# Batch 0's second transform step in two halves, its rows loaded in three parts, and more second products seeded by ScalarE

## The chip, the cores and the metric

One core of one Trainium2 chip. The metric is device time in microseconds (us) for one launch of the whole program; smaller is better.

## The reference

Eight batches of 4224 positions by 192 channels go through two stages. First a dynamic convolution: seven softmaxed taps per position and head, causal (six zero rows in front). Its output x then goes through a block with a Fourier mix and a normalised two-layer product:

```
mixed = real(fft(fft(x, axis=1), axis=2))
u  = x + mixed
un = (u - mean(u)) / sqrt(var(u) + 1e-6)
out = u + maximum(un @ w_ch1, 0) @ w_ch2      # 192 -> 768 -> 192
```

## The kernel before

**Tiles.** The 4224 positions are 33 rows of 128. A batch has nine groups, c or g: groups 0 to 7 hold four rows each, group 8 one row. All rows of a group sit on the 128 partitions.

**Convolution** (`conv`, batches 0 and 1; `wide_conv` from batch 2). Each of the seven taps of a group is one product, 128x768 (L810 on VectorE, L808 on GpSimd). In batch 0 the seven products of groups 0, 1, 3, 5 and 7 (`PE_SUMS`) are summed by TensorE, by matmuls with the identity into two PSUM banks `pa` (L815, and L772 for taps that ScalarE made in 24-column pieces, L763, as `ACT_TAPS` says); ScalarE copies the sums out (L689). The products of the other groups are added one at a time, by GpSimd (L822), in batch 1 the first of them by VectorE (`DVE_ADDS`).

**First transform step** (`fold`, `spectrum`). GpSimd folds a group's rows with their mirror rows into `sm` (L836, L837), TensorE multiplies by a table into `pg` (L845), ScalarE copies a part (`up`, L851), VectorE makes `gt` (L852, L855), and every second group SP stores `gt` to a DRAM tile `g_d` (L858, L859).

**Second transform step** (`transform`). When all of `g_d` is written, six loads of 112 partitions bring it back transposed as `g2` (L931, L933). 44 matmuls, 99 columns wide for all 17 row pairs, give `pp` (L941), and ScalarE copies each `pp` into `pq` in two or three pieces (L945, L951, L953, L956).

**Mix, norm, product** (`mix`, `norm`, `mlp`). Per group, four matmuls of 97 columns give an even part and an odd part in `eo` (L972); ScalarE copies the odd part (`ot`, L977), VectorE takes difference and sum (L978, L979) and adds both to `u` (L980, L981). The first three groups of batch 0 (`QUICK`) take a short path through normalisation: VectorE statistics, ScalarE scaling to `un` (L1018), TensorE transposes `tr` (L1028), casts to `ht`. Then comes the first product `ph` (L1105) with ReLU evictions `hh`, and the second product `po` (L1149). For the first six groups the second product is in float32, after that in three float16 terms. The end of a tile is either a VectorE instruction u = po * scale + u (L1158), or, from group 10 of the run and for the second tile only (`SEEDED`, `SEED_TILES`), a ScalarE "seed" that writes scaled u into the bank ahead of the matmuls (L1146) and a ScalarE eviction (L1156).

**Weights** arrive as 64-bit words; `words_to_f32` turns each of six pieces into float32 by seven VectorE instructions (L492 to L503), `prep_w1` and `split_f32` make float16 high and low parts.

**Order.** Every engine runs its queue in order. The order is not that of the program text: `plan` prices every instruction (`cost`) and walks through the whole graph; it repeats the walk with ranks from a backward walk (`TURNED`, `PARTS`) and keeps the best order for all five queues. Buffers are by tag: `po` 2 PSUM banks, `fft` 2, `ph` 3; `u` 8 tiles of SBUF. `keep_warm` issues spare matmuls: 40 after group 7 of batch 0 (`WARM`), 8 and 8 between the first mixes (`WARM_EO`).

Of the kernel before, what the change touches and what calls it, by code (L numbers as in the profile page):

```python
# [11 lines left out]
F16 = mybir.dt.float16  # L12
F32 = mybir.dt.float32
# [10 lines left out]
NK1 = 65  # L24
DH = 97
# [11 lines left out]
SPLIT = 4  # L37
# [8 lines left out]
WIRE = 0.7  # L46

F32_GROUPS = 6
WIDE_FROM = 2
SEEDED = 10  # L50
# [18 lines left out]
TURNED = 10  # L69
# [3 lines left out]
PARTS = (1.0, 0.9, 0.7, 0.5)  # L73
LAG = 1000
PATIENCE = {"dve": 120}
# [73 lines left out]
def cost(ins, lane, reads, writes):  # L149
# [10 lines left out]
    if lane == "sp":  # L160
        if ins.opcode == "DmaTransposeAnt":
            return TURN * n / (12 * P), 2000 + 1.2 * n, 1.09 * n
        size, run = BYTES[out.dtype], min(together(ap) for ap in reads + writes)
        return 400, 2000 + WIRE * count(out) * size, out.ap[0][1] * count(out) / run * (0.5 + 0.0023 * run * size)
# [3 lines left out]
    if lane == "pool":  # L168
        t = 183 + (1.92 if out.dtype == F16 else 2.13) * n
        return t - 45, t  # L170
    t = 190 + (0.833 if out.ap[-1][0] == 1 else 1.666) * n + 90 * (len(reads) - 1)
    return (t + 100, t + 90) if len(writes) > 1 else (t - 95, t)


def plan(nc, tc, homes, holds, glued, opening):
# [4 lines left out]
    for at, ins in enumerate(nc.cur_bb.bb.instructions):  # L180
# [14 lines left out]
        for name, spot, w in spots:  # L195
            kind, tag, bufs = homes[name]
            if name not in users and bufs and kind != "dram":
                rows[kind, tag].append(name)
            users[name].append(k)
# [27 lines left out]
    def walk(rank, rows, back=False):  # L227
# [7 lines left out]
        order, table, wire, streamed = {lane: [] for lane in HOP}, None, 0.0, False  # L235
# [17 lines left out]
        for _ in ops:  # L253
# [14 lines left out]
            if lane == "pe" and not back:  # L268
                if mixing[k] and streamed:
                    busy, done = busy - LOADED, done - LOADED  # L270
                streamed = streams[k]
            free[lane], end = now + busy, now + done
# [22 lines left out]
    best = now = walk(list(range(len(ops))), rows)  # L295
    for _ in range(TURNED):
        last = {name: max(now[1][k][1] for k in users[name]) for name in row_of}
        turned = walk([-end for _, end in now[1]], {row: sorted(names, key=lambda name: -last[name]) for row, names in rows.items()}, True)
        if turned is None:
            break  # L300
        late = [turned[0] - end for _, end in turned[1]]
        now = min((w for w in (walk([part * t + (1 - part) * s for t, (s, _) in zip(late, now[1])], rows) for part in PARTS) if w),
                  key=lambda w: w[0], default=None)
        if now is None:
            break
        best = min(best, now, key=lambda w: w[0])
    order = best[2]
# [22 lines left out]
def dft_tables(D):  # L330
# [12 lines left out]
    for kk in range(3):  # L343
        for v in range(N2):
# [6 lines left out]
    te, to = te.reshape(6 * NT, -1), to.reshape(6 * NT, -1)  # L351
    d = np.arange(DH, dtype=np.int64)
# [5 lines left out]
            for m in (f1, te, to, np.concatenate([cm, sm], axis=1))]  # L358
# [3 lines left out]
def tile_dynconv_fnet_mlp(  # L362
# [42 lines left out]
    cs_sb = cpool.tile([DH, 2, DH], F32, name="cs_sb")  # L405
# [3 lines left out]
    ones = cpool.tile([1, P], F32, name="ones")  # L409
    nc.vector.memset(ones, 1.0)  # L410
# [16 lines left out]

    g_ds = [dr.tile([NK1, 2, NT, D], F32, tag=f"g_d{i}", name=f"g_d{i}", bufs=1) for i in range(2)]

    def load_consts():  # L430
        zero = pq[0:NT].rearrange("p e r k -> p (e r k)")[:, 0:2 * D].rearrange("p (k d) -> p k d", k=2)
        nc.gpsimd.memset(zero, 0.0)
        for g_d in g_ds:
            nc.sync.dma_start(g_d[0:NK1:NK1 - 1, 1].rearrange("k t d -> t k d"), zero)
# [3 lines left out]
        nc.sync.dma_start(te_sb, te.rearrange("r (k c) -> r k c", k=3))  # L438
        nc.sync.dma_start(to_sb, to.rearrange("r (k c) -> r k c", k=3))
        csv = cs.rearrange("r (m c) -> r m c", m=2)  # L440
# [14 lines left out]
    def weight_scale(words, bits, nm, other=None):  # L455
# [8 lines left out]
        m2 = cpool.tile([1, 1], F32, name=f"m2_{nm}")  # L464
        row = pst("ph", 3, [P, P], F32, f"mr_{nm}")
# [19 lines left out]
    def words_to_f32(raw, out, nm, bank):  # L485

        hi, lo = raw[:, :, 1], raw[:, :, 0]
        v = nc.vector
        a = pst(*bank, [P, PW], I32, f"pa_{nm}")
        w = pst(*bank, [P, PW], F32, f"pw_{nm}")  # L490
        t = temp(f"t_{nm}", I32)
        v.tensor_scalar(out=a, in0=hi, scalar1=3, scalar2=0x3FFFFFFF,  # L492
                        op0=ALU.logical_shift_left, op1=ALU.bitwise_and)
        v.scalar_tensor_tensor(out=t, in0=hi, scalar=-0x40000000, in1=a, op0=ALU.bitwise_and, op1=ALU.bitwise_or)
        v.tensor_scalar(out=a, in0=hi, scalar1=0x7FF00000, scalar2=None, op0=ALU.bitwise_and)
        v.scalar_tensor_tensor(out=w, in0=a, scalar=float(0x38100000), in1=t.bitcast(F32),
                               op0=ALU.is_ge, op1=ALU.mult)
        v.tensor_scalar(out=a, in0=w.bitcast(I32), scalar1=23, scalar2=23,
                        op0=ALU.logical_shift_right, op1=ALU.logical_shift_left)
        r = t.bitcast(F32)  # L500
        ins = v.scalar_tensor_tensor(out=r, in0=lo.bitcast(U32), scalar=2.0 ** -52, in1=a.bitcast(F32), op0=ALU.mult, op1=ALU.mult)
        out = w if out is None else out
        last_word.append(v.tensor_tensor(out=out, in0=w, in1=r, op=ALU.add))  # L503
        return out
# [21 lines left out]
    def prep_w1(raws):  # L526
# [5 lines left out]
        with held(g2_loads[0, (NK1 + 2) // 3 // TRI * TRI].ins):  # L532
# [12 lines left out]
    def split_w2(_):  # L545
# [7 lines left out]
        for i, both in enumerate((fsc, isc)):  # L553
            nc.vector.tensor_tensor(out=both, in0=scales[0][:, i:i + 1], in1=s2[:, i:i + 1], op=ALU.mult)
# [10 lines left out]
    wm = cpool.tile([P, N2 * H], F32, name="wm")  # L565
# [60 lines left out]
    def conv(b):  # L626

        g_d = g_ds[b % 2]
# [53 lines left out]
        gt, tails, sums, ws_of, firsts = None, [], {}, {}, {}  # L682
        def finish(c, R, u, wp, pa, *_):

            nonlocal gt, done
            if pa:
                n = R * D // 2
# [3 lines left out]
            if R > 1:  # L691
# [625 lines left out]
```

## Time and profile before

| | us |
|---|---|
| median of 3 runs | 1078.33 (1078.23 to 1079.11) |
| span of the profiled execution | 1076.2 |
| what lies around the span, against the median | 2.1 |
| TensorE busy | 1057.1 (98%) |
| VectorE busy | 933.7 (87%) |
| ScalarE busy | 862.9 (80%) |
| GpSimd busy | 851.4 (79%) |

The profile is of one execution. A matmul's duration holds its latency, and matmuls are pipelined, so their rate is read from bursts: duration of a burst less that of one instruction, over the count less one. A float32 matmul of the program is two MATMUL instructions in the trace.

### The profile page before, as it was taken

The page shows a single profiled execution, that of the slowest core. Times are in us where ns is not written, and L with a number is a line of the kernel's source. Part 1 is how long each engine was busy: PE and PEld are TensorE (multiplying, and loading weights), DVE is VectorE, ACT ScalarE, POOL GpSimd, SP SyncE. Part 2 cuts the span into 40 slices and gives each one's busy share as a digit, 9 for nine tenths or more (in the row PEclk, how much of TensorE's full clock was granted, in tenths as well). Part 3 has the DMA queues.
Part 4 walks back from the last instruction along what each step waited for, and adds up shares of the span by engine and source line. Part 5 has one row for each costly group of instructions (what it writes and reads, how often), then busy time and mean ns, then how long its engine had stood idle before and what let it go on. Part 6 is the DMA issues. An engine that isn't in the chain of part 4 may idle for free.

```text
span 1076.2 us, 23645 instructions
## 1 busy us (share of the span) xinstructions
PE 1057.1 (98%) x8603; PEld 803.8 (75%) x8603; DVE 933.7 (87%) x1597; ACT 862.9 (80%) x2597; POOL 851.4 (79%) x616
## 2 busy tenths in 40 slices
PE   8899999999999999999999999999999999999998
PEld 5476687886778777887778777787778777886667
DVE  8999999999989998899989998899989997374433
ACT  4666875669987998889897898889897998699953
POOL 5979899899969999699959999699969999011210
PEclk9999999999999999999999999999999999999999
DMA  9453056624683458625582447734583424523221
GB/s 322 136 147 117 8 136 180 175 48 101 157 233 80 98 133 210 158 75 121 145 215 80 111 127 205 157 76 125 137 180 89 88 68 99 143 56 87 72 71 49
DMA packets 186324, 134.88 MB, mean 125 GB/s; under 512 B 134299, under 2 KB 167008, under 8 KB 186208
## 3 DMA queue, kind: packets, MB, share of 16 engines
q1 hardware_dynamic: 186208, 133.37, 48.3%
q8 instruction: 68, 1.11, 0.4%
q14 instruction: 48, 0.39, 0.1%
HBM read 61.46 MB, written 39.37 MB: 94 GB/s over the span
## 4 chain that ended last, share of the span: by engine, by line
PE 66%; POOL 15%; DVE 10%; issue 5%; ACT 2%; DMA 1%; SPq 0%; POOLq 0%; DVEq 0%; ACTq 0%
PE po L1149 28%; PE ph L1105 24%; POOL u L893 7%; POOL u L822 4%; PE pp L941 4%; PE eo L972 3%; PE ph L1072 3%; PE pg L845 3%; DVE pr L810 2%; POOL sm L836 2%; POOL hl L1048 1%; DVE pr L889 1%; DVE u L889 1%; DMA x_sb<-in_x_dram 1%; POOL hl L1050 1%
## 5 line engine op out<-in xcount | busy, mean ns | idle before, releaser
L893 POOL TENSOR_TENSOR u<-u,pr 128x1536 f32<-128x1536 f32 x144 | 497.1, 3454 | 15.4 <-DVE pr L889 13.4
L1149 PE MATMUL po<-w2h,hh 128*128 128x192 f16 x2880 | 411.2, 246 | 1.3 <-ACT po L1146 0.8
L1149 PEld LDWEIGHTS <-hh 128*128 128x128 f16 x4320 | 364.1, 98 | 61.6 <-issue 18.9
L1105 PE MATMUL ph<-ht,w1h 128*128 128x512 f16 (+1 forms) x1296 | 387.5, 362 | 2.6 <-DVE hh L1125 1.2
L1149 PE MATMUL po<-w2l,hh 128*128 128x192 f16 x1440 | 354.1, 246 | 0.0
L1125 DVE SCALAR_TENSOR_TENSOR hh<-ph,hh 128x512 f16<-128x512 f32 (+1 forms) x396 | 241.3, 634 | 77.5 <-ACT hh L1124 76.9
L889 DVE TENSOR_TENSOR pr<-x_sb,wp 128x1536 f32<-128x1536 f32 x144 | 250.2, 1743 | 6.8 <-POOL u L893 6.7
L1124 ACT ACTIVATE hh<-ph 128x512 f16<-128x512 f32 (+1 forms) x396 | 208.8, 551 | 48.5 <-PE ph L1105 27.1
L1105 PEld LDWEIGHTS <-w1h 128*128 128x128 f16 x1296 | 126.9, 100 | 94.8 <-issue 16.9
L1105 PE MATMUL ph<-ht,w1l 128*128 128x512 f16 (+1 forms) x528 | 180.4, 350 | 0.0
L1038 ACT ACTIVATE un<-u,rs 128x192 f32<-128x192 f32 x252 | 122.0, 539 | 16.4 <-POOL rs L1036 13.1
L1048 POOL TENSOR_TENSOR hl<-un,hl 128x512 f16<-128x512 f32 (+1 forms) x69 | 74.3, 1077 | 74.8 <-ACT hl L1042 39.5
L822 POOL TENSOR_TENSOR u<-u,pr 128x768 f32<-128x768 f32 (+1 forms) x72 | 115.6, 1612 | 8.8 <-DVE rs L1012 4.7
L1009 ACT ACTIVATE junk<-u,st 128x192 f16<-128x192 f32 x252 | 114.2, 453 | 3.0
L1007 ACT ACTIVATE junk<-u 128x192 f16<-128x192 f32 x252 | 90.8, 360 | 21.9 <-DVE u L981 17.5
L972 PEld LDWEIGHTS eo<-cs_sb,pq 97*128 97x128 f32 x544 | 93.4, 191 | 9.0 <-issue 1.1
L972 PE MATMUL eo<-cs_sb,pq 97*128 97x97 f32 x544 | 92.3, 265 | 0.1
L810 DVE TENSOR_TENSOR pr<-x_sb,wp 128x768 f32<-128x768 f32 (+1 forms) x91 | 74.6, 867 | 1.4 <-PE pa L815 0.7
L1105 PEld LDWEIGHTS <-w1l 128*128 128x128 f16 x528 | 52.9, 100 | 23.7 <-issue 3.7
L1036 POOL TENSOR_TENSOR rs<-st,rs 128x4 f32<-128x4 f32 (+1 forms) x69 | 14.0, 202 | 67.8 <-DVE rs L1012 63.1
L836 POOL TENSOR_TENSOR sm<-u 128x382 f32<-128x382 f32 x64 | 64.0, 1000 | 3.4 <-ACT u L689 3.2
L845 PE MATMUL pg<-sm,f_sb 128*128 128x192 f32 x256 | 55.1, 333 | 1.4 <-POOL sm L837 1.3
(143 smaller groups left out, 1585.5 us busy)
## 6 DMA issues: line engine op xcount, KB each, us to landing
out_dram<-u SPq DMA_DIRECT2D x64, 384.0 KB
x_sb<-in_x_dram SPq DMA_DIRECT2D x48, 384.0 KB
g<-g_d SPq DMA_DIRECT2D x40, 336.0 KB
x_sb<-in_x_dram SPq DMA_DIRECT2D x8, 864.0 KB
g_d<-gt SPq DMA_DIRECT2D x32, 195.0 KB
g_d<-gt SPq DMA_DIRECT2D x32, 189.0 KB
w<-in_weight_gen_dram SPq DMA_DIRECT2D x6, 924.0 KB
x_sb<-in_x_dram SPq DMA_DIRECT2D x8, 672.0 KB
```

The lines of the kernel that those rows point to most:

```text
L810: last_product[b] = nc.vector.tensor_tensor(out=dst, in0=rows, in1=wk, op=ALU.mult)
L822: adder.tensor_tensor(out=u, in0=u, in1=pr, op=ALU.add)
L889: last_product[b] = nc.vector.tensor_tensor(out=pr.rearrange("p (s r) (h g) -> p s (r h) g", s=2, g=G), in0=rows, in1=wp[:, :, :, k:k + 1] ...
L893: nc.gpsimd.tensor_tensor(out=u, in0=u, in1=pr, op=ALU.add)
L972: last_mix[b] = nc.tensor.matmul(eo[:, e, j, :], lhsT=pq[0:DH, e, r, r:r + P], rhs=cs_sb[:, e, :], start=True, stop=True)
L1007: nc.scalar.activation(junk, uv[t], AF.Identity, scale=-1.0 / D, accum_out=st[:, t, 0:1])
L1009: nc.scalar.activation(junk, uv[t], AF.Square, bias=st[:, t, 0:1], accum_out=st[:, t, 1:2])
L1038: nc.scalar.activation(un[:, t, :], uv[t], AF.Identity, bias=rs[:, 1, t:t + 1], scale=rs[:, 0, t:t + 1])
L1105: last_ph[n] = nc.tensor.matmul(ph[:, 0:T], lhsT=wt[:, cs_], rhs=ht[:, 0:T, blk], start=(i == 0 and not opens), stop=(i == len(terms) - 1 ...
L1124: nc.scalar.activation(a[:, 0:T], ph[:, 0:T], AF.Relu)
L1125: nc.vector.scalar_tensor_tensor(out=l[:, 0:T], in0=ph[:, 0:T], scalar=0.0, in1=a[:, 0:T], op0=ALU.max, op1=ALU.subtract)
L1149: nc.tensor.matmul(po[t // 2][:, t % 2, :], lhsT=hx[:, t], rhs=wx[:, c2, :], start=(c2 == 0 and i == 0 and not seeds[t // 2] and not (late ...
```

## The change

- The second step of batch 0 gets its own function. `g_d` of batch 0 is three DRAM tiles (`STAGES`: row pairs 0 to 8, 9 to 12, 13 to 16). Three loads per part bring its rows to 54, 24 and 24 partitions of the same three tiles (tag `u`); the first two parts are loaded once group 5 is stored, the last after group 7. Group 6 is stored by itself.
- The near half of the step makes the seven row pairs that the first three groups need: 44 matmuls of 39 columns into four banks, evicted by ScalarE (even) and VectorE (odd). The far half (44 matmuls of 60 columns, ScalarE evictions) stands behind the first three norms.
- Group 6 of batch 0 isn't folded on GpSimd, and group 7 is neither summed nor folded ahead of `pg`: TensorE multiplies the table with near rows, mirrored far rows and their first column, product by product (five pieces: two products, ScalarE's tap, and two sums of two products by VectorE). Its sum for `u` follows behind.
- The mix of the first three groups makes even plus odd on TensorE (194 columns, no copy, no difference and sum).
- `words_to_f32` has four VectorE instructions and two of ScalarE in place of seven of VectorE.
- Seeds from group 3 of the run (`SEEDED`); groups 3 to 9 seed both tiles (`SEED_BOTH`). `DVE_ADDS` gives VectorE a second add for groups 3, 5 and 7 of batch 1. ScalarE's taps: two for groups 1 and 3, one for 5 and 7. Fewer spare matmuls.
- `plan` runs a fixed list of walks with shaken ranks and takes the last; its costs for DMA and for a cold TensorE differ.

```diff
+STAGES = ((0, 9), (9, 13), (13, 17))
-PE_SUMS = {(0, 0), (0, 1), (0, 3), (0, 5), (0, 7)}
+PE_SUMS = {(0, 0), (0, 1), (0, 3), (0, 5)}
+DIRECT = {(0, 7)}
+PAIRS = 2
+ACT_PIECE = 2
+UNFOLDED = {(0, 6)}
-DVE_ADDS = {(1, c): 1 for c in range(2, NC)}
+DVE_ADDS = {(1, c): 1 + c % 2 for c in range(2, NC)}
-SEEDED = 10
+SEEDED = 3
+SEED_BOTH = 10
-ACT_TAPS = {(0, 1): (0,), (0, 3): (0,), (0, 5): (0,1), (0, 7): (0,)}
+ACT_TAPS = {(0, 1): (0, 1), (0, 3): (0, 1), (0, 5): (0,), (0, 7): (0,)}
-WARM = {-1: 14, 7: 40}
-WARM_EO = (8, 8)
+WARM = {-1: 14, 7: 8}
+WARM_EO = (4, 4)
...
-    best = now = walk(list(range(len(ops))), rows)
-    for _ in range(TURNED):
+    now = walk(list(range(len(ops))), rows)
+    for part, spread, seed in TRIALS:
+        shake = [spread * (r - 0.5) for r in draws(seed, len(ops))]
...
-        now = min((w for w in (walk([part * t + (1 - part) * s for t, (s, _) in zip(late, now[1])], rows) for part in PARTS) if w),
...
+        now = walk([part * t + (1 - part) * s + r for t, (s, _), r in zip(late, now[1], shake)], rows)
...
+            if (b, c) in DIRECT:
+                gt = spectrum(b, c, None, gt, pa)
+                banks = [pst("po", 2, [P, 512], F32, f"pa_{b}_{c}_{i}") for i in range(2)]
+                with held(last_pg[0].ins):
+                    for at, both in enumerate(pa):
+                        for bank, rows in zip(banks, both):
+                            nc.tensor.matmul(bank[:, 0:n], lhsT=ident32, rhs=rows.rearrange("p r d -> p (r d)"),
...
+        for i, both in enumerate(pieces or ()):
+            for j in range(J):
+                near, far = both[0][:, j, :], both[1][:, 1 - j, :]
+                parts = ((pg[:, j, :], near), (pg[:, j, 1:D], far[:, D - 1:0:-1]), (pg[:, j, 0:1], far[:, 0:1]))
...
+            if (b, c) == (0, 5):
+                for part in range(len(STAGES) - 1):
+                    load_early(part)
...
+    def load_early(part):
+        lo, hi = STAGES[part]
+        n, g_d = 6 * (hi - lo), g_0s[part]
+        for m0 in range(0, NM, 8):
+            nm = min(8, NM - m0)
...
+            last_g2[0] = nc.sync.dma_start(early[m0 // 8][6 * lo:6 * hi, 0:nm], bass.AP(first.tensor, first.offset, [[D, n], [n * D, nm], [1, D]]))
...
+    def transform_first():
...
+        load_early(len(STAGES) - 1)
...
+        n0 = 2 * QUICK + 1
+        c0, half = NT - n0, NM // 2
+        for m0 in range(0, NM, half):
...
+            for e, (tab, d0) in enumerate(tables):
+                pp = pst(("fft", "po")[e], 2, [P, 3 * half, 2 * n0 - 1], F32, f"pp_0_{m0}_{e}")
...
+                last_pq[0] = place(e, 0, k0, nk, src[:, n0 - 1:2 * n0 - 1], src[:, n0 - 1::-1], (("act", "act"), ("dve", "dve"))[e])
+        yield
+        n1 = NT - n0
+        for m0 in range(0, NM, 8):
...
+                pp = pst("fft", 2, [P, 24, 2, n1], F32, f"pp_0_{m0}_{e}_far")
...
+            if joined:
+                low = eo[:, 0, j, :]
+                where = bass.AP(low.tensor, low.offset, [low.ap[0], [(3 - 2 * j) * DH, 2], [1, DH]])
+                rhs = cs_sb[:, 1:3] if e else cs_sb[:, 0:1].broadcast_to([DH, 2, DH])
...
-                seeds = [late and (i in SEED_TILES or LT == 1) for i in range(2)]
+                seeds = [late and (i in SEED_TILES or LT == 1 or n - 1 < SEED_BOTH) for i in range(2)]
```

## Rows read from the trace of the kernel before

**Rows 1.** Page, part 1: span, and TensorE's share of it

```profile
span 1076.2 us, 23645 instructions
PE 1057.1 (98%) x8603; PEld 803.8 (75%) x8603; DVE 933.7 (87%) x1597; ACT 862.9 (80%) x2597; POOL 851.4 (79%) x616
```

**Rows 2.** Windows: busy us per engine (count), granted clock, DMA share, GB/s

```profile
99.00:300.00 201.00, 196.59 (x1377) 149.52 (x1377) 195.43 (x349) 154.34 (x456) 192.11 (x135) 1.00 0.44 116
300.00:1000.00 700.00, 698.24 (x6124) 537.94 (x6123) 619.13 (x1014) 605.00 (x1799) 572.47 (x400) 1.00 0.51 125
1000.00:1076.00 76.00, 72.90 (x669) 53.70 (x667) 27.22 (x49) 46.59 (x121) 6.84 (x12) 1.00 0.25 68
```

**Rows 3.** Timeline of TensorE: start us, duration us, line, shape, count, idle before

```profile
57.72 2.20 PE L815 MATMUL pa<-pr,ident 128*128 128x384 f32 x6
...
60.41 5.32 PE L815 MATMUL pa<-pr,ident 128*128 128x384 f32 x16
...
67.50 1.46 PE L845 MATMUL pg<-sm,f_sb 128*128 128x192 f32 x8
...
70.87 8.97 PE L563 MATMUL warm<-ident 128*128 128x128 f32 x78
79.69 0.85 PE L941 MATMUL pp<-te_sb,g 102*97 102x99 f32 x8
...
99.23 0.38 PE L1105 MATMUL ph<-ht,w1h 128*128 128x512 f16 x1 [0.56 <-ACT ht L1029]
```

**Rows 4.** The chain that ended last, 60 to 72 us: start us, us, what

```profile
63.10 1.81 POOL u L822
...
69.53 0.90 PE pg L845 x4
...
71.21 0.26 DVE gt L855
```

**Rows 5.** Timelines of VectorE, ScalarE, GpSimd and SP's queue, 60 to 93 us

```profile
62.54 0.95 DVE L810 TENSOR_TENSOR pr<-x_sb,wp 128x768 f32<-128x768 f32 x1 [0.34 <-PE pa L815]
...
92.55 0.56 DVE L980 TENSOR_TENSOR u<-u,eo 128x388 f32<-128x388 f32 x1
...
89.96 0.25 ACT L953 ACTIVATE pq<-pp 97x68 f32<-97x68 f32 x1
...
72.90 1.54 POOL L808 TENSOR_TENSOR u<-x_sb,w 128x768 f32<-128x768 f32 x1 [3.50 <-DVE w L733]
...
71.85 0.32 SPq L859 DMA_DIRECT2D g_d<-gt  x1
75.44 10.26 SPq L931 DMA_DIRECT2D g<-g_d  x6
```

**Rows 6.** Groups by line and shape: count, busy us, mean ns, idle before

```profile
L1149 PE MATMUL po<-w2h,hh 128*128 128x192 f16 x2880 | 411.2, 246 | 1.3 <-ACT po L1146 0.8 <-DVE hh L1125 0.5
...
L822 POOL TENSOR_TENSOR u<-u,pr 128x768 f32<-128x768 f32 x60 | 108.6, 1817 | 5.9 <-DVE rs L1012 4.7
...
L845 PE MATMUL pg<-sm,f_sb 128*128 128x192 f32 x256 | 55.1, 333 | 1.4 <-POOL sm L837 1.3
...
L815 PE MATMUL pa<-pr,ident 128*128 128x384 f32 x120 | 44.0, 511 | 5.6 <-DVE pr L810 5.5 <-POOL pr L808 0.2
...
L941 PE MATMUL pp<-te_sb,g 102*97 102x99 f32 x336 | 37.9, 251 | 0.3 <-ACT pq L956 0.2
...
L1158 DVE SCALAR_TENSOR_TENSOR u<-po,isc,u 128x384 f32<-128x384 f32 x61 | 37.1, 608 | 14.5 <-PE po L1149 14.1
...
L1146 ACT ACTIVATE po<-u,fsc 128x384 f32<-128x384 f32 x55 | 31.9, 580 | 8.7 <-DVE u L1158 8.3
...
L498 DVE TENSOR_SCALAR pa_w<-pw_w 128x384 int32<-128x384 int32 x6 | 3.4, 560 | 0.1
```

**Rows 7.** Windows around a pause of TensorE early in the run, columns as in rows 2

```profile
8.00:11.00 3.00, 0.51 (x2) 0.38 (x3) 2.35 (x7) 2.11 (x11) 1.90 (x3) 1.00 1.00 409
11.00:15.00 4.00, 4.00 (x9) 2.21 (x8) 4.00 (x5) 3.45 (x18) 1.85 (x4) 0.57 1.04 404
```

More of the change, by code (lines that the diff above doesn't have):

```diff
@@ L72 @@
 NEAR = 1500
-PARTS = (1.0, 0.9, 0.7, 0.5)
 LAG = 1000
+COLD = 2600
+WINDOW = 5000
 PATIENCE = {"dve": 120}
@@ L271, in walk @@
                 streamed = streams[k]
+            if lane == "pe" and not back:
+                if now > free[lane] + COLD:
+                    slow = now + WINDOW
+                if now < slow:
+                    busy, done = 2 * busy, done + busy
             free[lane], end = now + busy, now + done
@@ L681, in conv @@
             return
-        gt, tails, sums, ws_of, firsts = None, [], {}, {}, {}
+        gt, tails, sums, ws_of, firsts, kept = None, [], {}, {}, {}, []
         def finish(c, R, u, wp, pa, *_):
             nonlocal gt, done
+            n = R * D // 2
+            if (b, c) in DIRECT:
[5 more added lines that the diff above has]
+                            nc.tensor.matmul(bank[:, 0:n], lhsT=ident32, rhs=rows.rearrange("p r d -> p (r d)"),
+                                             start=(at == 0), stop=(at == len(pa) - 1))
+                for i in range(2):
+                    nc.scalar.copy(u[:, i].rearrange("p r d -> p (r d)"), banks[i][:, 0:n])
+                done += R
+                return done / N2
             if pa:
-                n = R * D // 2
                 for i in range(2):
@@ L811, in conv @@
                         products.append(last_product[b].ins)
-                    if pa:
+                    if direct:
+                        pa.append((pr[:, 0], pr[:, 1]))
+                        left = K - len(at) - len(kept)
+                        if left % 2 == 0 and left < 2 * PAIRS:
+                            pa.pop()
+                            both, more = (q.rearrange("p r d -> p (r d)") for q in kept[-2:])
+                            nc.vector.tensor_tensor(out=both, in0=both, in1=more, op=ALU.add)
+                    elif pa:
                         n = R * D // 2
@@ L837, in fold, with spectrum @@
         last_fold[b] = nc.gpsimd.tensor_tensor(out=sm[:, :, 0], in0=a[:, :, 0], in1=z[:, ::-1, 0], op=ALU.add)
-    def spectrum(b, c, sm, gt):
-        J, g_d = (2 if c < NC else 1), g_ds[b % 2]
+    def spectrum(b, c, sm, gt, pieces=None):
+        J = 2 if c < NC else 1
         t2 = 2 * c + 1 if c < NC else 0
-        pg = pst("po" if (b, c) == (1, 0) else "fft", 2, [P, 2, D], F32, f"pg_{b}_{c}")
-        for j in range(J):
+        bank = ("po", 2) if (b, c) == (1, 0) else ("ph", 3) if (b, c) in DIRECT else ("fft", 2)
+        pg = pst(*bank, [P, 2, D], F32, f"pg_{b}_{c}")
+        for i, both in enumerate(pieces or ()):
+            for j in range(J):
+                near, far = both[0][:, j, :], both[1][:, 1 - j, :]
+                parts = ((pg[:, j, :], near), (pg[:, j, 1:D], far[:, D - 1:0:-1]), (pg[:, j, 0:1], far[:, 0:1]))
+                for n, (dst, rows) in enumerate(parts):
+                    last_pg[b] = nc.tensor.matmul(dst, lhsT=f1_sb[:, t2 + j, :], rhs=rows, start=(i + j + n == 0),
+                                                  stop=(i == len(pieces) - 1 and n == 2), skip_group_check=True)
+        for j in range(J if not pieces else 0):
             last_pg[b] = nc.tensor.matmul(pg[:, j, :], lhsT=f1_sb[:, t2 + j, :], rhs=sm[:, j, :], start=True, stop=True)
@@ L1205, in queue @@
                 f(arg)
-    add(0.0, 1.0, transform(0))
-    run()
+    first_half = transform_first()
+    next(first_half)
     with held(last_up[0].ins):
```

218 lines of the change are left out of this document (142 added, 76 removed).

## The prediction

> **What bounds the kernel now.** I read the page's busy shares first [rows 1]: TensorE is busy for 98% of the span, no other engine for over 87%. A busy share can hide stages, so the windows come next [rows 2]. From 99 us on TensorE is idle for 4.4 us up to 300, for 1.8 us in the next 700, and for 3.1 us in the last 76: 9.3 us in all. What stands ahead of 99 us is the opening, in which TensorE mostly serves others: the first matmul of the first product starts at 99.23 [rows 3]. So the time is the opening plus the matmul work behind it plus some 9 us of gaps. An edit pays if it brings that first matmul forward, and costs what matmul work it puts behind it. Work taken off VectorE or GpSimd pays only where TensorE waits for them, and between 99 and 300 us they are busy for 195.4 and 192.1 of 201 us, so they are near the bound there too.
>
> The sum is made against the profiled execution, span 1076.2 us; the median of the runs, 1078.33, lies 2.1 above it, which I add unchanged.
>
> **The opening, term by term.** The marks of before are: last `gt` done 71.47 [rows 4], second step's loads issued from 75.44 [rows 5], first `pp` 79.69 [rows 3], last copy into `pq` done 90.21, first add to `u` 92.55 [rows 5], first product 99.23.
>
> *Last gt.* Three engines end close together. VectorE's last product ends at 63.49 and GpSimd's last sum (group 6) at 64.91; then come the folds and group 7's `pg`, 69.53 to 70.43 [rows 4, 5]. That looks like 5 us to be had by dropping folds. But TensorE works without a pause to speak of from 57.72 [rows 3]. From a burst, less one instruction's own duration [rows 3, 6], a sum instruction comes every (5.32 - 0.51)/15, about 0.33 us, four per product, so the seven products of group 7 cost 28 x 0.33 = 9.2 us; a 192-column one of `pg` every (1.46 - 0.33)/7 = 0.16 us, a 128-column one 8.97/78 = 0.115 us. A piece of the new group 7 is two tiles of four wide instructions and two of one column. For one column I take 0.115 us, as for 128 (below, nothing; above, the 0.16 of 192 columns). That is 2 x (0.64 + 0.23) = 1.7 us, five of them 8.7. Group 6 unfolded adds 1.7 - 0.65 = 1.1. So TensorE's work here stays: -9.2 + 8.7 + 1.1 = +0.6. It starts some 0.9 us sooner (one product fewer for VectorE in groups 1 and 3 each, one more in 5), and about 0.8 us of the wait for copy and fold goes. Term -1.1. Bounds: 0, if TensorE's queue takes it all, and -3.5, if it clears early and group 6 binds (64.91, piece 1.7, then the same 1.04 from `pg` to `gt`, about 67.9). The two pair sums (2 x 0.95) lie in place of the waits for a bank before products [rows 5].
>
> *Store to load.* 75.44 - 71.47 = 3.97 us. Half the bytes in the last store: between 3.0 and 4.0, I take 3.5, as the wait is mostly not bytes. Term -0.5.
>
> *Load to first pp.* 4.25 us, with 336 KB per load and several in flight. Now three loads of 147 KB or less; parts one and two went ahead. Between 2.2 and 4.25 I take 3.25. Term -1.0. On SP's queue the six early loads (0.33 us each, 2 us) wait for group 5's store and stand near the last stores; a slip there costs up to 2 us, which is kept for the range. The Trainium skill ("DMA: Bandwidth & Descriptors", the section on why a DMA increments its semaphore by 16) says that a DMA from SP uses the largest number of engines up to 16 that divides its outer size. By that, 24 rows run on 12 engines, 54 on 9, against 16 for 112 rows. This speaks against the parts: as an estimate, a third more time for the moving bytes would take half of this term, for a total 0.5 us higher.
>
> *Second step.* 79.69 to 90.21, 10.5 us. Its 88 instructions of 99 columns come every (0.85 - 0.25)/7 = 0.086 us [rows 3, 6], 7.6 us, and the rest is waiting for loads and for ScalarE to free two banks. With 39 columns the spacing lies between 0.034 (in proportion) and 0.086 (if something other than columns sets it); I take 0.06: 5.3 us. Four banks, so no wait for one. The last eviction adds about 0.7 (two copies; 0.25 us for 68 elements [rows 5], some 0.35 for 230); even and odd go out on two engines. 6.0 us, term -4.5 (bounds -6.8 and -2.2).
>
> *Mix of group 0.* From the last copy to the first add, 2.34 us, with a copy, a difference and a sum between. Now eight instructions of 194 columns, at 0.168 each 1.3 us, part of them ahead of the last eviction, and straight into the add. Term -1.1, and -0.2 for instructions of group 1 that no longer stand between. Weight preparation loses three VectorE instructions of 0.56 us on each of six pieces [rows 6], 10 us; with them in place it would have held this start, so it is a condition, not a term.
>
> Sum of the opening: -1.1 - 0.5 - 1.0 - 4.5 - 1.3 = -8.4; the first product starts near 90.8.
>
> **Behind the start.** The far half is another 88 instructions. 60 columns: between 0.052 and 0.086 us, I take 0.06, 5.3 us. Joined mixes add 24 x (0.168 - 0.115) = 1.3. Sixteen fewer spare instructions between the mixes give back 16 x 0.115 = 1.8. Net TensorE work +4.8 from the second step on. All of it counts, because the wait for the norm shrinks as well and has no other gap left.
>
> Costed at nothing, with their cover: 13 VectorE endings of 0.61 us become 26 ScalarE instructions of 0.58 (groups 3 to 9), 15 us on ScalarE, which has 47 us idle between 99 and 300 [rows 2, 6]; without it each seed would stop TensorE. Three adds of 1.82 us go from GpSimd to VectorE [rows 6], covered by what VectorE loses (8 us of endings, weight work). Far evictions, 14 copies of some 0.35 us, go to the same idle time of ScalarE. The sum of group 7 (20 x 0.33 = 6.6 us) and 8 spare pairs fill the DMA wait, where 78 spare instructions, 9 us, stand now [rows 3]. Steady batches 2 to 7 are unchanged but for their order.
>
> 1078.3 - 8.4 + 4.8 = **1074.7 us**.
>
> **Rivals.**
> - *Batch 1's rows hold the gain.* TensorE comes to batch 1 sooner, but GpSimd, busy for 192 of 201 us, starts that batch's sums at 72.90 for VectorE's tap tables [rows 2, 5]. If that start stays, it gains only the three adds, 5.4 us, which would do; if VectorE is late with them, none, and the 3.6 us become waits: 1076 to 1078.3, say 1077. For: the near-full window. Against: VectorE is relieved more than it is given. Chance 0.15.
> - *The opening clears early.* `gt` at the -3.5 bound and spacing by columns: -2.4 and -2.3 more, 1070.0. For: folds and copies really go from the chain. Against: TensorE's unbroken run from 57.72. Chance 0.2.
> - *Seeds stop TensorE; slower.* A bank must now be evicted, seeded and handed over before the first matmul of a tile. The one such wait of before took 0.8 us [rows 6]. If all 13 new seeds cost that, +10.4: 1085. It decides from 5 such waits on (+4, gain gone). Against: 55 seeds cost 0.8 us together. Chance 0.08.
> - *The clock falls in the DMA wait.* After TensorE had worked 0.51 of 3 us, the granted clock was 0.57 over the next 4 us [rows 7], the lower level of 1.2 GHz for most of them. If it falls ahead of the near half, that and the first mix double, +6.6: 1081. The Trainium skill ("TensorE: Matmul & The Clock Gate", the part on the HAM clock gate) says that the slow level is the default and that activity lifts it; the trace agrees. Against: 6.6 us of sums plus spare work in that wait. Chance 0.04.
> - *It doesn't do what it says*: a part's loads or SP's order hold the near half, so load and step gain nothing but columns: about +2, 1076.7. Chance 0.08.
>
> **How the numbers follow.** The forecast has the rest, 0.45, with 1072 to 1076.2 as its own range. A measurement of this kernel tells about 0.2%, 2.2 us, from no change: below 1076.2 is faster, above 1080.5 slower. Faster: most of the forecast, the early case and a small part of the others, 0.74. Same: most of batch 1's hold and of the case where loads don't come early, with the forecast's upper tail, 0.16. Slower: seeds and clock with part of their tails, 0.10. Range 1067 (early case with a cheap far half) to 1079 (the holds with a slip on SP's queue).
>
> **What the changed profile would show.** Right: first product near 91; a near half of about 6 us; store to first `pp` under 7.2 us in place of 8.2; no pause of TensorE before seeded tiles; idle after the start still near 9 us. Last `gt` before 68 speaks for the early case, after 71 against my first term. Wrong: a first product later than 95, over 13 us of idle between 99 and 300, or a granted clock below 1.00 behind 60 us.

## The result, and the profile after

The changed kernel takes 1085.87 us (median of four runs, 1084.76 to 1088.02), against 1078.72 for the kernel before in the same session: ratio 1.007, 95% interval 1.0056 to 1.0085. It is 0.7% slower, clear of the noise, and outside the range that was given. The profiled execution took 1088.02 us with a span of 1086.2, and the sums below are made against that span; it is the slowest of the four, so they overstate the median's loss by some 2 us.

First the timeline of TensorE (start, duration, line, shape, count, idle time before it):

```profile
79.96 0.38 PE L506 MATMUL me_w<-m_w,ones_w 1*128 1x1 f32 x2
82.47 14.54 PE L1016 MATMUL pp<-first_tables,g 102*97 102x39 f32 x88 [2.13 <-issue]
97.69 5.25 PE L1111 MATMUL eo<-cs_sb,pq 97*128 97x194 f32 x16 [0.68 <-ACT pq L1028]
...
103.44 1.48 PE L1111 MATMUL eo<-cs_sb,pq 97*128 97x194 f32 x8
...
108.45 2.96 PE L1016 MATMUL pp_far<-first_tables,g 102*97 102x60 f32 x32
...
112.00 1.51 PE L1016 MATMUL pp_far<-first_tables,g 102*97 102x60 f32 x16
113.35 0.38 PE L1247 MATMUL ph<-ht,w1h 128*128 128x512 f16 x1
...
114.83 1.32 PE L1016 MATMUL pp_far<-first_tables,g 102*97 102x40 f32 x14
```

Three things stand against [rows 3]. The first `pp` starts at 82.47, not 79.69, behind a pause of 2.1 us that was not there before. The near half takes 14.54 us, 0.16 us per instruction, almost twice what its twin, the far half, takes in the same trace (2.96 us for 32). And sixteen joined mixes take 5.25 us, while the next eight take 1.48. The windows say why (columns as in [rows 2]; the granted clock is the third column from the right):

```profile
60.00:80.00 20.00, 19.70 (x111) 16.06 (x109) 14.51 (x29) 9.75 (x34) 15.18 (x11) 1.00 0.60 179
82.00:84.00 2.00, 1.53 (x10) 1.56 (x10) 1.61 (x4) 0.57 (x1) 2.00 (x2) 0.51 1.04 221
84.00:90.00 6.00, 6.00 (x39) 6.00 (x38) 0.00 (x0) 2.57 (x7) 6.00 (x5) 0.50 0.89 293
90.00:97.00 7.00, 7.00 (x44) 6.88 (x43) 2.65 (x7) 1.02 (x2) 7.00 (x5) 0.50 0.04 9
98.00:102.00 4.00, 4.00 (x13) 4.00 (x13) 2.61 (x6) 2.34 (x6) 4.00 (x4) 0.50 0.00 0
103.00:200.00 97.00, 95.74 (x596) 75.66 (x595) 92.98 (x192) 71.89 (x200) 77.86 (x63) 1.00 0.32 94
```

From 82 to 102 TensorE runs at the lower level, 1.2 GHz; between its first pause, which is like that of [rows 7], and 1085 us it does so nowhere else. In this run the clock fell at the pause, ahead of the near half. Note that the busy column says 6.00 of 6 and 7.00 of 7: a busy share doesn't show a halved clock.

GpSimd's last sum of group 6 and VectorE's last `gt` come late already (67.8 and 72.2 us):

```profile
65.34 2.46 POOL L883 TENSOR_TENSOR u<-u,pr 128x768 f32<-128x768 f32 x1
...
71.85 0.34 DVE L924 TENSOR_TENSOR gt<-pg,up 128x190 f32<-128x190 f32 x1
```

The rest of the late rows is on SP's queue and in the chain of waits. Both are shown around the last stores (the first fence is SP's timeline, the second the chain):

```profile
72.22 0.30 SPq L933 DMA_DIRECT2D g<-gt  x1
72.97 0.27 SPq L934 DMA_DIRECT2D g<-gt  x1
73.61 2.80 SPq L1010 DMA_DIRECT2D g<-g  x3
...
78.66 1.16 SPq L1010 DMA_DIRECT2D g<-g  x3
```

```profile
67.56 6.03 DMA g<-gt
...
73.61 0.30 SPq L1010
...
73.96 6.48 DMA g<-g
80.44 2.02 issue
```

The last store is issued at 72.97 and the loads that need it at 78.66, 5.7 us later; before it was 71.85 and 75.44 [rows 5], 3.6 us. The store of group 5 lands 6.03 us after its issue. What ran beside these stores are the early loads. The chain names a load of part two and leaves the 2.02 us behind it open ("issue"). By the steps of the loads' semaphores, which the trace also records, it is part three's first load, issued at 78.66, that lands last ahead of the first `pp`, at 82.27.

What did go well stands behind the first mix:

```profile
99.00:300.00 201.00, 197.63 (x1392) 155.95 (x1391) 188.78 (x348) 160.07 (x462) 177.50 (x128) 0.99 0.38 99
300.00:1000.00 700.00, 699.44 (x6164) 544.89 (x6163) 621.73 (x1027) 607.61 (x1818) 582.10 (x402) 1.00 0.51 129
1000.00:1086.00 86.00, 83.19 (x748) 60.34 (x745) 31.43 (x56) 54.82 (x146) 8.82 (x15) 1.00 0.25 65
```

TensorE's idle time is 3.4, 0.6 and 2.8 us, together 6.8 where [rows 2] had 9.3, and GpSimd has 177.5 us of work in the first window where it had 192.1.

### The profile page after: what moved, and what is told of

The parts are those of the page before. It is cut to its first block, busy times and chain, and to the rows that moved or that the text cites. A ratio compares the mean times of both kernels' runs of the same rounds, so it can differ in the third digit from the quotient of the medians.

```text
span 1086.2 us, 23835 instructions
## 1 busy us (share of the span) xinstructions
PE 1066.8 (98%) x8667; PEld 824.3 (76%) x8667; DVE 917.8 (84%) x1566; ACT 881.0 (81%) x2657; POOL 847.7 (78%) x611
## 4 chain that ended last, share of the span: by engine, by line
PE 81%; DVE 9%; DMA 3%; POOL 3%; ACT 2%; issue 2%; SPq 0%; POOLq 0%; ACTq 0%
PE po L1292 33%; PE ph L1247 29%; PE eo L1111 5%; PE pp L1055 5%; PE ph L1214 4%; PE pg L914 3%; DVE pr L864 3%; POOL u L883 2%; DVE pr L967 2%; PE pp L1016 1%; DVE hh L1267 1%; DMA x_sb<-in_x_dram 1%; PE pp_far L1016 1%; ACT pr L809 1%; DMA g<-g 1%
## 5 line engine op out<-in xcount | busy, mean ns | idle before, releaser
L1292 PE MATMUL po<-w2h,hh 128*128 128x192 f16 x2880 | 423.5, 246 | 0.0
L1292 PEld LDWEIGHTS <-hh 128*128 128x128 f16 x4320 | 368.8, 98 | 65.4 <-issue 16.5
L1247 PE MATMUL ph<-ht,w1h 128*128 128x512 f16 (+1 forms) x1296 | 393.7, 362 | 1.9 <-DVE hh L1267 1.8
L883 POOL TENSOR_TENSOR u<-u,pr 128x768 f32<-128x768 f32 (+1 forms) x69 | 111.6, 1622 | 22.7 <-issue 15.2
L1190 POOL TENSOR_TENSOR hl<-un,hl 128x512 f16<-128x512 f32 (+1 forms) x69 | 74.3, 1077 | 57.5 <-issue 28.2
L1111 PEld LDWEIGHTS eo<-cs_sb,pq 97*128 97x128 f32 x544 | 101.9, 195 | 9.4 <-ACT pq L1028 0.8
L1111 PE MATMUL eo<-cs_sb,pq 97*128 97x97 f32 (+1 forms) x544 | 99.1, 271 | 0.8 <-ACT pq L1028 0.7
L864 DVE TENSOR_TENSOR pr<-x_sb,wp 128x768 f32<-128x768 f32 (+1 forms) x84 | 68.3, 860 | 2.1 <-POOL u L883 1.2
```

What stands on the lines that cost most here:

```text
L864: last_product[b] = nc.vector.tensor_tensor(out=dst, in0=rows, in1=wk, op=ALU.mult)
L883: adder.tensor_tensor(out=u, in0=u, in1=pr, op=ALU.add)
L1111: last_mix[b] = nc.tensor.matmul(where, lhsT=pq[0:DH, e, r, r:r + P], rhs=rhs, start=not joined or e == 0, stop=not joined or e == 1)
L1247: last_ph[n] = nc.tensor.matmul(ph[:, 0:T], lhsT=wt[:, cs_], rhs=ht[:, 0:T, blk], start=(i == 0 and not opens), stop=(i == len(terms) - 1 ...
L1292: nc.tensor.matmul(po[t // 2][:, t % 2, :], lhsT=hx[:, t], rhs=wx[:, c2, :], start=(c2 == 0 and i == 0 and not seeds[t // 2] and not (late ...
```

## The experiments

In all but the thin spares and the last two, the order of all engines is that of the changed kernel but for the edit named; spare matmuls and moves on SP are put in behind the planner. Times of before in these sessions were 1078.3 to 1078.6.

**A bridge over the pause.** If the pause lowered the clock, work in it should keep it.

```diff
+ for _ in range(10):   # ahead of the first matmul of the near half
+     nc.tensor.matmul(warm_bank, lhsT=ident32, rhs=ident32)
```

> The changed kernel with ten more spare 128-column matmuls of TensorE right ahead of the near half, every other instruction in the same order. They fill the pause of 2.13 us (80.34 to 82.47) behind which the granted clock fell to 0.50 for 20.5 us. Theory A, the clock costs the time: clock 1.00 from 14 us on, near half about 7.3 us in place of 14.5, first mix 2.7 in place of 5.3, time 1074 to 1078, below the kernel before. Theory B, the loss lies in the new order and work behind the opening: the time stays within 2 us of the changed kernel's 1085.9 even if the clock holds. Theory A2, the pause does not matter, because the near half's 39-column matmuls alone lose the clock: it falls a few us into the near half, time 1080 to 1086.

Measured: 1083.77 us, ratio to before 1.0046 (1.0029 to 1.0063). The near half, and windows:

```profile
82.30 10.57 PE L1024 MATMUL pp<-first_tables,g 102*97 102x39 f32 x88
```

```profile
80.00:86.00 6.00, 6.00 (x65) 6.00 (x65) 3.30 (x10) 1.90 (x6) 6.00 (x5) 1.00 1.04 280
87.00:92.00 5.00, 5.00 (x33) 5.00 (x33) 1.77 (x5) 1.31 (x3) 5.00 (x4) 0.50 0.40 94
```

The pause is gone and the clock falls all the same, inside the near half. So the pause decides when it falls, not that it falls. This is the third theory, A2. The near half, at full clock for its first part, takes 10.57 us in place of 14.54.

**The loads of x later.** Five loads of batch 1's rows that stood behind the last parts go behind the weight copies on SP.

```diff
- g2 loads, x_sb loads, w1 copies
+ g2 loads, w1 copies, x_sb loads
```

> The changed kernel with five loads of x for batch 1 moved on SP's queue from ahead of the eight small copies of the first weights to behind them; no other instruction moves. In the changed kernel they were issued from 79.87 us, while the last rows of the second step were still landing (82.27). If these loads hold up the rows: first matmul of the near half 1 to 2 us earlier, at 80.5 to 81.5, the pause of TensorE under 1.2 us, and the clock may stay at 1.00, then 1075 to 1079. If the rows are held up by their own packets or engines: first near-half matmul within 0.4 us of 82.47, clock lost as before, 1084 to 1088.

Measured, one execution: 1083.37 us; the first `pp` starts at 81.40, 1.1 us sooner, and the clock still falls. Some 0.4 us of that are there already at the last stores (71.80 in place of 72.22), so about 0.7 us are the loads': those of the next batch took some part in holding the rows up.

**Thin spares in the kernel before.** In the kernel before, the spare matmuls of the DMA wait move one column instead of 128.

```diff
- nc.tensor.matmul(spare, lhsT=ident32, rhs=ident32)
+ nc.tensor.matmul(spare[:, 0:1], lhsT=ident32, rhs=ident32[:, 0:1])
```

> The kernel before with its 40 spare matmuls ahead of the second step cut from 128 columns to one column; same number, same order. TensorE issues just as many instructions there but streams next to nothing. If instructions alone keep the clock: granted clock 1.00 throughout, time within 2 us of 1078.5. If the clock needs the columns: it falls to 0.50 between 74 and 80 us, the second step of the kernel before takes longer than its 10.5 us, and the time rises by 3 to 10 us, to 1082 to 1088: that is then the price of the clock in the old structure.

Measured, one execution: 1085.11 us beside 1078.58 for before. The windows, and below them that of the kernel before over the same wait:

```profile
60.00:72.00 12.00, 11.75 (x54) 8.15 (x52) 10.52 (x25) 10.30 (x40) 7.21 (x9) 1.00 0.39 136
73.00:80.00 7.00, 7.00 (x35) 7.00 (x34) 6.90 (x19) 0.58 (x1) 7.00 (x5) 0.50 0.62 165
```

```profile
72.00:80.00 8.00, 8.00 (x75) 8.00 (x74) 7.90 (x21) 0.90 (x3) 7.10 (x5) 1.00 0.63 167
```

This is the clearest of all: TensorE is issued without a gap, 35 instructions in 7.00 of 7 us, and the clock is halved, where the kernel before, busy for 8.00 of 8 us, keeps 1.00. The weights are 128 columns wide in both; the spares move one column in place of 128. The price in the old structure is 6.5 us, but it doesn't lie where the expectation looked for it. The timeline of the run:

```profile
75.70 10.38 PE L564 MATMUL warm<-ident 128*128 128x1 f32 x48
85.94 1.61 PE L942 MATMUL pp<-te_sb,g 102*97 102x99 f32 x8
...
96.90 2.21 PE L973 MATMUL eo<-cs_sb,pq 97*128 97x97 f32 x16
```

At the lower level the one-column spares take about 0.22 us each (10.38 over 48), against 0.115 for 128 columns at full clock [rows 3], and the second step, which stands behind them in the queue, starts at 85.94 in place of 79.69: 6.2 us. From there to the first mix it is only 1.0 us longer (10.96 in place of 9.94).

**Columns into the near half.** Ten spares as above, the loads of x later, and behind every second matmul of the near half a spare of 83 columns into the unused end of its bank.

```diff
  for i, mm in enumerate(second_step(pp, rows_of, near, d0, m0, half)):
+     if i % 2 == 1:
+         nc.tensor.matmul(bank[0:83, 429:512], lhsT=ident32[:, 0:83], rhs=ident32[:, 0:83])
```

> The changed kernel with ten spare matmuls ahead of the near half, a spare matmul of 83 columns behind every second one of the near half's 44 (20 in all, into unused columns of the same banks), and the five loads of x moved behind the weight copies on SP. The rest of the order is as it was. Clock theory: the pause alone was not the cause, the near half itself is (39 columns moved for 97 columns of weights leave TensorE idle inside). With the spares in it the granted clock stays at 1.00; the near half takes 88 x 0.083 + 40 x 0.072 = 10.2 us in spite of the added work, the first mixes 2.9 us in place of 5.3 to 5.5; first ph near 106, time near 1080.7. Rival, rows that land late or something else but the clock sets the near half's pace: near half 10.6 + 2.9 = 13.5 us, mixes as before, time 1085 or more.

Measured: 1081.68 us, ratio 1.0026 (1.0015 to 1.0036). Start and end of the near half, and windows:

```profile
82.47 0.46 PE L1032 MATMUL pp<-first_tables,g 102*97 102x39 f32 x4
...
92.64 0.46 PE L1032 MATMUL pp<-first_tables,g 102*97 102x26 f32 x4
```

```profile
80.00:93.00 13.00, 13.00 (x150) 12.97 (x150) 5.88 (x17) 4.20 (x10) 13.00 (x9) 1.00 0.53 140
94.00:97.00 3.00, 3.00 (x10) 3.00 (x10) 1.94 (x5) 2.42 (x6) 3.00 (x3) 0.50 0.35 135
```

The near half with 40 more instructions in it takes 10.6 us, at full clock, where the changed kernel takes 14.54. The bridge alone gave 10.57, so inside the near half the spares cost what they save; what they add is that the clock is still high at its end. It falls for about 3 us behind the wait before the first mix, so it did not stay at 1.00 throughout. The clock theory's sums come near (it had 10.2 us and 1080.7), and the rival's 13.5 us and 1085 fall.

**Partitions of the parts.** The parts padded to 64, 32 and 32 partitions, with zero rows in the tables.

```diff
- early[m0 // 8][6 * lo:6 * hi, 0:nm], bass.AP(..., [[D, n], [n * D, nm], [1, D]])   # n = 54, 24, 24
+ early[m0 // 8][p0:p1, 0:nm], bass.AP(..., [[D, p1 - p0], [n * D, nm], [1, D]])     # 64, 32, 32
```

> The changed kernel with the three parts of the rows padded to 64, 32 and 32 partitions (zero rows in the tables), so 18 to 33% more bytes per load; order of all engines as it was. Theory that the number of partitions of a load (54 and 24) keeps DMA engines idle: the store of group 5 lands in under 5.5 us in place of 6.0, the last rows 1 to 2 us earlier than 82.3, time 1083 to 1085. Rival, latency and the waits in SP's queue set it, not the spread over engines: last rows at 82 or later, time 1085.5 to 1087.

Measured: 1085.54 us, ratio 1.0062 (1.0047 to 1.0077). With 18 to 33% more bytes the last parts are issued at 77.34 in place of 78.66 and the first `pp` starts at 81.49 in place of 82.47. That is what the first theory wants of the rows, but the time isn't told apart from that of the changed kernel. It leans to the theory and settles nothing.

**Where the loads stand on SP.** Two runs. In the first the two loads of part one that stand between the stores go behind the last store; in the second only the last six loads are turned to go tile by tile. Here p2.t0 is part two's load into the first of the three tiles; p1.t0 goes ahead of all of these.

```diff
- stores g4/5, p1.t1, p1.t2, stores g6, stores g7, p2.t0, p2.t1, p2.t2, p3.t0, p3.t1, p3.t2
+ stores g4/5, stores g6, stores g7, p2.t0, p1.t1, p2.t1, p3.t0, p3.t1, p1.t2, p2.t2, p3.t2      (first run)
+ stores g4/5, p1.t1, p1.t2, stores g6, stores g7, p2.t0, p3.t0, p2.t1, p3.t1, p2.t2, p3.t2      (second run)
```

> The changed kernel with the two loads of the first part that stand between the stores moved behind the last store, and all loads behind it in the order of the tiles. Theory that the early loads slow the stores down: the store of group 5 lands in 3 to 4 us in place of 6.0, first pp at 79.5 to 80.5 in place of 82.5, and the time falls by as much, 1083.5 to 1084.5, with the clock still low in the near half. Rival, stores land late for their own reasons (many small packets): first pp at 82 or later and the time within 1 us of 1085.9.

> The changed kernel with the six last loads on SP turned from part two (three tiles), part three (three tiles) to tile by tile: the first tile's part two and part three, then the second tile's, then the third's. Nothing else moves. Theory that the loads of part two that run beside the last store hold it up (5.4 us to landing in the changed kernel, 2.9 us in the run where no loads ran beside it): now one load of part two runs beside it, the first tile's part three is issued near 76.5 in place of 78.7 and the first pp starts at 80 to 81 in place of 82.5; time 1083.5 to 1084.5, the clock still low in the near half. Rival, the store lands late whatever runs beside it, or the rows land late for the bytes ahead of them: first pp at 82 or later, time 1085.5 to 1086.5.

Measured: 1086.55 us (1.0076, 1.0061 to 1.0091) and 1085.64 us (1.0069, 1.0054 to 1.0083). SP's timeline of the first run:

```profile
72.68 0.32 SPq L945 DMA_DIRECT2D g<-gt  x1
73.53 1.93 SPq L1021 DMA_DIRECT2D g<-g  x3
...
75.62 1.99 SPq L1021 DMA_DIRECT2D g<-g  x5
```

The load that waits for the last store is issued 2.9 us after it, not 5.7. So the loads of part one did hold the store up. But its tile now queues behind three other loads, it lands 7.1 us after its issue in place of 3.6 (by its semaphore), and the first `pp` starts at 82.82: what was won at the store was lost at the bytes ahead. In the second run the wait for the store stays (72.71 to 77.95), so part two is not what held it. The first `pp` starts at 81.19, then waits 0.5 us in the half. Each theory was half right.

**All repairs.** Loads tile by tile, x later, two spares ahead, twelve in the near half (behind every third matmul), four in the wait before the first mix. The second run of this kind also moves part one's two loads behind the first tile's last part.

```diff
+ stores g4/5, p1.t1, p1.t2, stores g6, stores g7, p2.t0, p3.t0, p2.t1, p3.t1, p2.t2, p3.t2      (first run)
+ stores g4/5, stores g6, stores g7, p2.t0, p3.t0, p1.t1, p2.t1, p3.t1, p1.t2, p2.t2, p3.t2      (second run)
```

> All repairs together on the changed kernel: loads tile by tile as in the run before, the loads of x behind the weight copies, two spare matmuls ahead of the near half, one spare of 83 columns behind every third matmul of the near half (12), and four in the wait before the first mix. Theory that clock and late rows are the whole loss: first pp near 80.3, near half 7.3 + 12 x 0.144 = 9.0 us, first mix at 90, granted clock 1.00 (or low for 4 us at most), first ph near 103.3 and with 972.6 us behind it a span near 1076, time 1077 to 1078.5: at or below the kernel before. Rival, that the two-half step is slower by itself: time over 1080 with the clock at 1.00 throughout.

> The run with all repairs, but the two loads of part one that stand between the stores go behind the last store too, and behind the first tile's loads: first tile part two, part three, then the second tile's three parts, then the third's. Theory that the loads of part one, 54 partitions and 0.58 MB, are what holds the last store up (landing 5.4 us after issue with them, 2.9 without): first tile's part three is issued near 75.6 and the first pp starts near 80, 1.5 us sooner than in the run before; with the clock at 1.00 time 1078.5 to 1079.5. Rival, the same bytes now come behind the store and the near half waits for the second and third tile: first pp sooner, but waits of 1 us or more inside the near half and no gain, 1080 or more.

Measured: 1081.84 us (1.0046, 1.0025 to 1.0068) and 1078.94 us (0.9999, 0.9988 to 1.0011). The first is not steady: six of its twelve executions took 1079.2 to 1080.8, two about 1083 and four 1087.5 to 1089.8, at a mean granted clock of 0.989 to 0.991 in those four. Its profiled execution took 1080.43 us at a mean clock of 0.998, but the first `pp` still waited for its rows until 81.47; so its expectation, 1077 to 1078.5, was missed. The second took 1078.3 to 1080.0 in all ten, as expected, at 0.997 to 1.00. TensorE's timeline of the second, SP's and the windows:

```profile
80.69 0.63 PE L1041 MATMUL pp<-first_tables,g 102*97 102x39 f32 x6
...
89.97 0.80 PE L1111 MATMUL pp<-ident 128*83 128x83 f32 x8
90.80 2.90 PE L1145 MATMUL eo<-cs_sb,pq 97*128 97x194 f32 x16
...
104.19 0.38 PE L1281 MATMUL ph<-ht,w1h 128*128 128x512 f16 x1
```

```profile
72.43 0.32 SPq L959 DMA_DIRECT2D g<-gt  x1
...
74.51 3.29 SPq L1035 DMA_DIRECT2D g<-g  x7
```

```profile
80.00:90.00 10.00, 10.00 (x119) 9.98 (x119) 5.85 (x17) 4.18 (x10) 10.00 (x8) 1.00 0.46 100
90.00:100.00 10.00, 9.86 (x83) 9.36 (x83) 9.97 (x39) 7.20 (x19) 10.00 (x7) 1.00 0.51 183
```

The load that waits for the last store is issued 2.1 us after it, the first rows are there when TensorE's spare work ends, and the clock stays at 1.00. The same three groups of loads in another order and 18 spare matmuls take the whole loss away, and no more than that.

**Rows in time, no spares.** The same order on SP, not one spare matmul added.

> The changed kernel with the loads moved as in the last run of all repairs (five loads of part one and two behind the last store, first tile first; x behind the weight copies) and not one spare matmul added. Theory that the 39-column near half lowers the clock by itself, pause or not: TensorE runs into the near half at 80.3 with no pause to speak of, the granted clock falls 2 to 6 us into it all the same, near half 10 to 12 us, first mixes at half speed, first ph near 107, time 1081.5 to 1083.5, so 3 to 4.5 us are the clock's where the rows are in time. Rival, the clock falls only behind a pause of TensorE: clock 1.00 throughout, near half 7.3 us, no spares to pay for, time 1076.5 to 1077.5, faster than both kernels.

Measured: 1083.21 us (1.004, 1.0029 to 1.0052). Timeline and windows:

```profile
79.84 0.38 PE L519 MATMUL me_w<-m_w,ones_w 1*128 1x1 f32 x2
80.15 1.74 PE L1029 MATMUL pp<-first_tables,g 102*97 102x39 f32 x18
82.17 8.70 PE L1029 MATMUL pp<-first_tables,g 102*97 102x39 f32 x70 [0.29 <-issue]
91.54 4.90 PE L1124 MATMUL eo<-cs_sb,pq 97*128 97x194 f32 x16 [0.68 <-ACT pq L1041]
```

```profile
80.00:85.00 5.00, 4.71 (x54) 4.61 (x54) 3.69 (x11) 2.52 (x7) 5.00 (x4) 1.00 0.55 126
86.00:91.00 5.00, 4.87 (x30) 4.74 (x30) 1.57 (x5) 1.12 (x3) 5.00 (x4) 0.50 0.49 123
```

TensorE runs into the near half without a pause worth the name (0.29 us in it) and the clock falls in it, as expected. With the near half as it is the clock falls with or without a pause ahead of it; the rival would have given 1076.5 to 1077.5. The last run of all repairs differs from this one by its 18 spares alone, and they are worth some 4 us: 1078.94 in place of 1083.21, with 1078.52 and 1078.58 for before in their sessions.

**Two controls with a new order.** The first is the kernel before with only the seeds of the change; the second the changed kernel with the old second step in one piece and everything else kept. Both change the count of operations, so the planner orders everything anew.

```diff
- SEEDED = 10                                                  (on the kernel before)
+ SEEDED = 3; SEED_BOTH = 10
```

```diff
- first_half = transform_first(); next(first_half)             (on the changed kernel)
+ add(0.0, 1.0, transform(0)); run()      # one DRAM tile, six loads of 112 partitions
```

> The kernel before (its own second step, no parts, its own planner) with only the seeds of the change: from group 3 of the run, both tiles for groups 3 to 9. The planner makes a new order. Theory that the seeds are worth something behind the start: the opening stays (first ph 98 to 101), TensorE's idle time between 99 and 300 us falls from 4.4 to 2 or 3, time 1076 to 1077.5. Rival, TensorE is bound by its own work and idle time goes elsewhere: 1078 to 1079. Seeds that stop TensorE: over 1081, with idle time before the second product's matmuls.

> The changed kernel with the second step of batch 0 as it was before, in one piece of 99 columns with six loads of 112 partitions and one DRAM tile; everything else of the change stays (group 7 multiplied product by product, group 6 unfolded, joined mixes, shorter weight preparation, seeds from group 3, two added adds on VectorE). Two spare matmuls more ahead of it. The planner makes a new order from nine walks. Theory that halves and parts are what costs, and the rest is worth 2 to 3 us: last gt at 71 to 72.5, first pp near 80, granted clock 1.00 behind 15 us, first ph near 98, idle of TensorE behind it 7 us or less, time 1075 to 1077. Rival, the rest of the change is worth nothing without the halves, or only in the order that was chosen for it: 1078 to 1081.

Measured: 1085.97 us (1.0069, 1.0052 to 1.0086) and 1080.93 us (1.0023, 1.0014 to 1.0033). Neither tells what it was made for. In the first, TensorE waits near 190 us for a weight that VectorE makes late in the new order, and the clock falls there as well (wait, then window):

```profile
PE ph L1106 <- DVE w2l L553: 3.8, 1, 3.8
```

```profile
192.00:199.00 7.00, 5.81 (x15) 2.86 (x15) 6.09 (x11) 2.86 (x5) 4.92 (x9) 0.52 0.66 198
```

In the second the same weight costs 2.3 us, in the profiled run with no such fall; by its number it falls to its rival (1078 to 1081). An order found for other work isn't a control. What the seeds or the rest are worth by themselves stays open.

## Why the prediction was wrong, step by step

The forecast span was 1076.2 - 8.4 + 4.8 = 1072.6, the measured one 1086.2, 13.6 more. Cut at two marks (the forecast's marks are 79.69 - 2.6 = 77.1, and 6.0 us behind that):

| us | before | forecast | after | all repairs |
|---|---|---|---|---|
| start to first `pp` | 79.69 | 77.1 | 82.47 | 80.69 |
| first `pp` to first mix | 9.94 | 6.0 | 15.22 | 10.11 |
| first mix to end | 986.6 | 989.5 | 988.5 | 987.1 |

The forecast's second mark is the last copy into `pq`, which in before ends 0.6 us behind the start of the first mix. Of the 13.6 us, 5.4 lie ahead of the first `pp`, 9.2 between it and the first mix, and the rest came out 1.0 us under the forecast.

- **The clock rival, given a chance of 0.04, is what happened.** It cost 14.54 - 7.5 = 7.0 us in the near half and 5.25 - 2.90 = 2.35 in the first mixes, 9.4 together (7.5 is 88 times the 0.085 of the far half, 2.90 the mixes at full clock in the repaired run). With the rows in time and no spares it still cost 10.7 - 7.5 = 3.2 and 4.90 - 2.90 = 2.0 us. The rival's sum was +6.6. Its mechanism was half right: it looked for idle time in the DMA wait and found cover there, and as the rows came late, the cover ran out and a pause of 2.1 us did come; but without the pause the clock falls too, in the middle of a near half that TensorE works through without a gap. The step that failed is the sentence against it, "6.6 us of sums plus spare work in that wait", which looked at the time ahead of the near half and not at the near half itself.
- **The rows came 5.4 us later than forecast.** Last `gt` was done at 72.2, not 70.4: GpSimd's last sum of group 6 ended at 67.8, where before it ended at 64.9, and 22 instructions of `pg` stood behind it. This is outside the bounds of that term, which held that GpSimd's sums would end as before. Store to load took 6.5 us from the last `gt`, not 3.5; the forecast took the early loads to have gone ahead. Those of part one were in the store's way, and those of part two were issued behind it (73.61). The slip "of up to 2 us" on SP's queue was looked for in issue time; it lay in the transfers. Load to first `pp` took 3.8, not 3.25. So the rival "It doesn't do what it says", given 0.08, came true as well: the parts' loads held the near half, by 3.5 us in these two terms where it had about 2.
- The sentence from the Trainium skill ("DMA: Bandwidth & Descriptors", the section on why a DMA increments its semaphore by 16) spoke against the parts and was priced at 0.5 us. The run with 64 and 32 partitions agrees in direction (rows 1.0 us sooner with more bytes). The steps in which a load's semaphore rises agree with the counts of engines: behind one at the issue there are 12 for 24 partitions and 9 for 54, and there are 16 in all for 112, 64 or 32.
- **Spacing of the second step.** Taken as 0.06 us, it is 0.085 in the far half ((1.51 - 0.25)/15 to (2.96 - 0.25)/31) with 60 columns, (1.32 - 0.25)/13 = 0.082 with 40, and (1.74 - 0.25)/17 = 0.088 with 39 in the run of rows in time, before the clock falls; so it does not go by columns here: the upper bound, 0.086, was the value, 2.2 us more in each half. Before, 99 columns cost the same 0.086 [rows 3, 6]: two halves load the same weights twice, and the split of the columns saves nothing.
- **Behind the first mix** the forecast was too dear. With 2.35 of clock and 2.2 of spacing taken out, the rest is 5.6 us under it. 2.5 of that are idle time (9.3 to 6.8), which the forecast kept whole. The other 3 or so lie between the first mix and the first products, and were not taken apart. The mark "first product near 90.8" failed for one more reason: the forecast put the far half behind the first product, and in the trace 64 of its 88 instructions stand ahead of it. It starts at 113.35, and at 104.19 with all repairs.
- **With all repairs** the span is still 5.3 us over the forecast: 3.6 ahead of the first `pp`, 4.1 between it and the first mix (2.2 of spacing, some 1.9 of spares), and 2.4 under it behind. So the gain that was forecast is not there with the two losses taken away either.
- The other rivals fell. The opening did not clear early. Batch 1's rows held nothing, with GpSimd 15 us lighter. No seed stopped TensorE: the second product has no idle time ahead of it (the last number of this line).

```profile
L1292 PE MATMUL po<-w2h,hh 128*128 128x192 f16 x2880 | 423.5, 246 | 0.0
```

The list of what would prove it wrong named a granted clock below 1.00 behind 60 us and a first product later than 95, and both lines showed it at once. A last `gt` after 71 was to speak against the first term, and it did.

## What to carry to other kernels

Before a wide matmul is split by columns, measure its spacing at both widths: where it is the same, as for 99 and 39 columns here, each half costs as much as the whole. And look at the granted clock behind every change that makes matmuls narrow, since neither idle time nor a busy share shows it. A load that is issued early helps only if it doesn't hold up a store that later loads wait for; move it on the queue and look at the store's landing.

## What was not expected of the hardware

The granted clock was 0.50 with TensorE busy 7.00 of 7 us on one-column matmuls, and stayed at 1.00 in a near half of 39 columns once a spare of 83 columns stood behind every second or third matmul. Ten spares put into the pause made the near half behind them 4 us shorter (10.57 in place of 14.54): the clock then fell inside it and not ahead of it. Twelve spares in the near half kept the clock in ten executions of ten with one order of the loads, and with another it fell in at least four of twelve, so these repairs are near an edge. A version with fewer spares in the repaired order was not tried.
